# Moving an activation table's load behind the square root, telling a static schedule when stores land, and splitting the last stores over two queues

## The chip, the cores and the metric

The kernel runs on one core of one Trainium2 chip. The metric is the device time of one execution in microseconds (us). Its engines are TensorE (PE in the profile; PEld for its weight loads), VectorE (DVE), ScalarE (ACT), GpSimd (POOL) and SyncE (SP), which here issues DMAs. Each runs its own instructions in program order and waits for the others through semaphores.

## The reference

An attention block of the RWKV kind gives `x` (3072 tokens of 384 features); a normalised SwiGLU block follows. Only the second part matters here:

```python
rms = np.sqrt(np.mean(x * x, axis=-1, keepdims=True) + 1e-06)
xn = x / rms * rms_g
g = xn @ w_gate
silu = g * (1.0 / (1.0 + np.exp(-g)))
val = xn @ w_val
return (silu * val @ w_out).astype(np.float32)
```

So for each block of tokens a square root is wanted once, and SiLU many times.

## The kernel before

The sequence is cut into 12 chunks, s = 0 to 11, and from the third on two are handled together. The kernel does not issue instructions in the order in which it is written. It first collects operations with an estimated cost, then places them with a list scheduler that knows each engine's order and the dependences, and issues them in the order of the planned starts. `land` is the time that passes after an operation until its result may be used. For the part up to about 240 us a random search over deadlines, with fixed seeds, looks for a good plan.

```python
def hop(self, before, after):
    a, b = self.ops[before][0], self.ops[after][0]
    return self.ops[before][4] + (self.HOP if a != b or a == "SP" else 0.0)   # [4] is land
...
for seed in range(4):
    rng, best, goals = random.Random(seed), None, dict(first)
```

ScalarE's square root and SiLU need different tables. The instruction that loads a table is put in by the compiler, ahead of the first activation that needs it:

```python
add("ACT", 3.1, [key], ["diag"],
    lambda bank=bank: act.activation(rms, bank[:, 0:NT], AF.Sqrt, scale=1.0 / DM, bias=eps), name=f"sqrt {s}")
```

The steady part is made of groups of seven matmul products, f1 to f7, in the PSUM banks a, b and c. SiLU reads bank a after f5; the next group's f1 may overwrite bank a only when VectorE's product h0 has read it too:

```python
mm(xs_b, a_keys, a, lambda: wb[i][:, o], lambda: xb[s], False, "f5")
add("ACT", 0.38, ["sums"] + a_keys, ["g0"], lambda: act.activation(late["gv"][:, 0, 0], a[:, 0, 0:NT], AF.Silu), name="silu0")
add("DVE", 0.42, a_keys + ["g0"], [f"h{m}.0"], lambda: dve.tensor_mul(h[:, 0], a[:, 1, 0:NT], late["gv"][:, 0, 0]), name="h0")
```

Beside this, ScalarE checks that all weights lie in a range ("look"). A check loads raw weights into half of `rows_out`, the buffer in which the results of the second layer wait for their stores, and runs two activations on them. So its load has to wait until an earlier store has read the buffer:

```python
keys = [f"r{2 * turn['look'] + i}" for i in range(2)]
add("SP", 0.95, [], keys, lambda: sp.dma_start(out=raw, in_=...), land=2 * LAND, name=f"look {n}")
add("ACT", 0.57, [], keys, lambda: act.activation(hi, hi, AF.Abs), name=f"look {n}")
add("ACT", 0.81, [], keys + ["seen"], lambda: act.activation(hi, hi, AF.Relu, ..., accum_out=seen[:, n : n + 1]), ...)
```

The stores themselves, and the flag `bad` that every engine reads at the end to branch around a general version of the kernel:

```python
queue, issue = ("ACT", act) if k > 1 and s + 2 == NS else ("SP", sp)
...                                       # give(): two DMAs, one for each half of the partitions
add(queue, 1.2, [f"r{k}"], ["stored"], give, name="store")
...
add("DVE", 0.2, [key], ["bad"], lambda: dve.tensor_copy(bad, bank[0:1, 0:1]), name="flag")
add("ACT", 0.6, ["bad", "stored"], [], load, name="flag")
```

## Time and profile before

| | before |
|---|---|
| time, median of the first 3 runs | 633.1 us |
| TensorE busy / waiting | 610.8 / 15.9 us |
| waits of TensorE before 60, 60 to 260, 260 to 600, after 600 us | 7.26, 1.56, 6.31, 0.80 |
| from the end of VectorE's last addition to the end | 5.96 us |

The waits are the idle times of TensorE in front of each of its matmuls, added up. (The view of waits leaves out idle times up to 0.15 us; the sums have them.) In the profile a line names first the group or instruction, then its busy time, and behind the last bar or in brackets the idle time of the engine before it and what ended that idle time. "PE bank_a <- DVE h" is TensorE, about to write bank_a, waiting for VectorE's instruction that writes h. The group of table loads, from the groups of ScalarE by form, with count, busy time, mean duration in ns, and idle time before:

```profile
L92 ACT ACT_TABLE_LOAD x22 | 28.2, 1283 | 4.8 <-PE bank_a L92 3.7 <-PEq L1661 0.8
```

There are 22 loads of 1.28 us each: one at the start, and one in front of each change between square root and SiLU.

### The profile page before, as it was taken

Reading aid. Unit: us, or ns where it says so; the run is one execution under the profiler, and the core shown is the slowest. Engines: PE = TensorE matmul, PEld = TensorE weight load, DVE = VectorE, ACT = ScalarE, POOL = GpSimd, SP = SyncE. Lnnn points to the kernel's source line nnn. Section 1 sums busy time; section 2 is a strip of 40 time slices with the busy share of each in tenths; the row PEclk is TensorE's granted clock in tenths of the full one; section 3 lists DMA queues with packets and bytes.
Section 4 is the critical chain, followed back from the end, with each engine's and each line's share of the span. In section 5 each row is a group of like instructions: output and inputs, shape, how many; then the busy total and the mean of one; then the engine's idle time right before and its main releaser. Section 6 shows DMA issues by size and latency. Waiting matters only on the chain.

```text
span 633.1 us, 15313 instructions
## 1 busy us (share of the span) xinstructions
PE 610.8 (96%) x6540; PEld 538.8 (85%) x6540; DVE 439.5 (69%) x621; ACT 353.2 (56%) x895; POOL 42.0 (7%) x41
## 2 busy tenths in 40 slices
PE   8979999999999999999999899999899999899995
PEld 8867787866888899888899788899788899788995
DVE  7787888798865797667795447896456876355641
ACT  6794878276495343945965552877443773232200
POOL 2243323200000000000000000000000000000000
PEclk9998999999999999999999899999999999999999
DMA  8676743115510312352311514131434011300001
GB/s 295 220 273 205 236 141 110 69 56 153 198 33 26 100 48 77 81 188 71 94 68 40 161 52 151 40 119 32 125 102 127 32 35 33 100 26 2 1 13 44
DMA packets 22782, 62.92 MB, mean 99 GB/s; under 512 B 3152, under 2 KB 10160, under 8 KB 21296
## 3 DMA queue, kind: packets, MB, share of 16 engines
q1 hardware_dynamic: 22128, 61.46, 30.8%
q8 instruction: 53, 0.87, 0.6%
q10 hardware_dynamic: 576, 0.39, 0.3%
q14 instruction: 25, 0.20, 0.1%
HBM read 55.94 MB, written 4.72 MB: 96 GB/s over the span
## 4 chain that ended last, share of the span: by engine, by line
PE 84%; ACT 6%; DMA 5%; DVE 3%; issue 1%; SPq 1%; ACTq 0%; DVEq 0%
PE bank_b L92 27%; PE bank_a L92 24%; PE bank_c L92 22%; PE at L92 10%; DMA out_dram<-rows_out 2%; DMA rows_out<-in_wot_dram 1%; ACT MO L92 1%; ACT ME L92 1%; DMA TOK<-in_tok_dram 1%; DVE rows_out L92 1%; DMA chan<-in_chan_dram 1%; SPq L92 1%; ACT L92 1%; DVE h L92 0%; ACT ulp L92 0%
## 5 line engine op out<-in xcount | busy, mean ns | idle before, releaser
L92 DVE TENSOR_TENSOR gv<-bank_b,m 128x512 f32<-128x512 f32 x90 | 62.1, 690 | 71.5 <-PE bank_b L92 67.4
L92 ACT ACTIVATE rows_out<-rows_out 128x384 f32<-128x384 f32 x72 | 40.0, 556 | 33.7 <-DMA rows_out<-in_wot_dram 14.9
L92 PE MATMUL bank_a<-xa,wa 64*128 64x256 f32 x396 | 50.7, 389 | 6.6 <-DVE h L92 6.6
L92 PE MATMUL bank_b<-xa,wa 64*128 64x256 f32 x444 | 54.6, 378 | 0.9 <-DVE gv L92 0.9
L92 ACT ACTIVATE gv<-gv 128x512 f32<-128x512 f32 (+1 forms) x60 | 30.6, 521 | 35.2 <-DVE gv L92 34.8
L92 PEld LDWEIGHTS bank_a<-xa,wa 64*128 64x128 f32 x396 | 37.8, 189 | 14.2 <-DVE h L92 8.3
L92 DVE TENSOR_TENSOR gv<-bank_c,gv 128x512 f32<-128x512 f32 x60 | 41.4, 691 | 12.1 <-PE bank_c L92 11.0
L92 PE MATMUL bank_a<-wo,h 128*128 128x192 f32 (+1 forms) x264 | 49.4, 343 | 0.0
L92 ACT ACTIVATE ME<-dmask,du 64x64 f32<-64x64 f32 x176 | 46.2, 331 | 4.4 <-DVE du L92 3.7
L92 PEld LDWEIGHTS bank_b<-xa,wa 64*128 64x128 f32 x444 | 42.4, 187 | 7.3 <-DVE gv L92 1.7
L92 PE MATMUL bank_a<-xb,wb 64*128 64x256 f32 x396 | 48.2, 376 | 0.0
L92 ACT ACTIVATE MO<-dmask,du 64x64 f32<-64x64 f32 x176 | 46.6, 336 | 0.8
L92 PEld LDWEIGHTS bank_a<-wo,h 128*128 128x128 f32 x264 | 43.5, 190 | 3.6 <-issue 0.3
L92 ACT ACTIVATE gv<-bank_a 128x256 f32<-128x256 f32 x30 | 11.5, 383 | 60.7 <-PE bank_a L92 60.5
L92 PE MATMUL bank_b<-t,wb 64*128 64x256 f32 x360 | 45.0, 382 | 0.0
L92 PE MATMUL bank_b<-t,s 64*128 64x256 f32 x360 | 44.8, 382 | 0.0
L92 PE MATMUL bank_c<-t,s 64*128 64x256 f32 x360 | 44.5, 379 | 0.3 <-DVE rows_out L92 0.3
L92 PE MATMUL bank_c<-xb,s 64*128 64x256 f32 x360 | 43.9, 376 | 0.0
L92 PEld LDWEIGHTS bank_a<-xb,wb 64*128 64x128 f32 x396 | 38.3, 187 | 4.4
L92 ACT COPY m<-bank_a 128x512 f32<-128x512 f32 (+1 forms) x35 | 19.9, 568 | 37.8 <-PE bank_a L92 37.0
L92 PEld LDWEIGHTS bank_c<-t,s 64*128 64x128 f32 x360 | 34.3, 187 | 6.4 <-issue 1.2
L92 PEld LDWEIGHTS bank_b<-t,s 64*128 64x128 f32 x360 | 35.2, 190 | 4.4
(152 smaller groups left out, 1257.4 us busy)
## 6 DMA issues: line engine op xcount, KB each, us to landing
chan<-in_chan_dram SPq DMA_DIRECT2D x11, 1024.0 KB, 5.1
TOK<-in_tok_dram SPq DMA_DIRECT2D x11, 768.0 KB, 5.1
VS<-in_vpad_dram SPq DMA_DIRECT2D x24, 256.0 KB, 4.0
raw<-in_wot_dram SPq DMA_DIRECT2D x8, 576.0 KB, 4.6
rows_out<-in_wka_dram SPq DMA_DIRECT2D x12, 384.0 KB, 3.2
rows_out<-in_wkb_dram SPq DMA_DIRECT2D x12, 384.0 KB, 3.3
rows_out<-in_wot_dram SPq DMA_DIRECT2D x12, 384.0 KB, 3.3
out_dram<-rows_out SPq DMA_DIRECT2D x42, 96.0 KB, 2.3
```

Source lines behind the costliest of these rows:

```text
L92: return lambda *args, **kwargs: self.tc.keep_in_program_order(give(*args, **kwargs))
```

## The change

The intent has three parts: (1) a SiLU of one column right behind each square root, so that SiLU's table is loaded there and not in front of the first SiLU that TensorE waits for, with a plan that knows that the square root's result is ready 1.5 us before the pair ends; (2) a landing time of 2.5 us for stores in the plan; (3) each of the last block's stores split over SyncE's and ScalarE's queues, and the flag written behind the last addition.

```diff
+    TABLE = 1.5
+    def silu_table():
+        act.activation(spare, eps, AF.Silu)
...
-            add("ACT", 3.1, [key], ["diag"],
-                lambda bank=bank: act.activation(rms, bank[:, 0:NT], AF.Sqrt, scale=1.0 / DM, bias=eps), name=f"sqrt {s}")
+            def roots(bank=bank):
+                act.activation(rms, bank[:, 0:NT], AF.Sqrt, scale=1.0 / DM, bias=eps)
+                silu_table()
+            add("ACT", 3.3, [key], ["diag"], roots, land=-TABLE, name=f"sqrt {s}")
...                                       # likewise for the square root of two columns of s == 0
-            add(queue, 1.2, [f"r{k}"], ["stored"], give, name="store")
+            if s + 2 == NS:
+                add("SP", 0.6, [f"r{k}"], ["stored"], lambda: give((0,), sp), land=2.5, name="store")
+                add("ACT", 0.6, [f"r{k}"], ["stored'"], lambda: give((1,), act), land=2.5, name="store")
+            else:
+                add("SP", 1.2, [f"r{k}"], ["stored"], lambda: give((0, 1), sp), land=2.5, name="store")
...
-        add("DVE", 0.2, [key], ["bad"], ...)
-        add("ACT", 0.6, ["bad", "stored"], [], load, name="flag")
+        add("DVE", 0.2, [key, "r1"], ["bad"], ...)
+        add("ACT", 0.6, ["bad"], [], load, name="flag")
```

More of the change, by code (lines that the diff above doesn't have):

```diff
@@ L858, in mixing @@
             )
-            add(
-                "ACT", 3.1, [key], ["diag"],
-                lambda bank=bank: act.activation(rms, bank[:, 0:NT], AF.Sqrt, scale=1.0 / DM, bias=eps), name=f"sqrt {s}",
-            )
+            def roots(bank=bank):
+                act.activation(rms, bank[:, 0:NT], AF.Sqrt, scale=1.0 / DM, bias=eps)
+                silu_table()
+            add("ACT", 3.3, [key], ["diag"], roots, land=-TABLE, name=f"sqrt {s}")
             add("DVE", 1.75, [], ["diag"], lambda: dve.reciprocal(rms, rms), name=f"inv {s}")
@@ L871, in mixing @@
             if quick:
-                add("ACT", 0.3, [key], ["ms"], lambda bank=bank: root(bank, ms[:, 0]), name=f"sqrt {s}")
+                add(
+                    "ACT", 0.3 + TABLE, [key], ["ms"], lambda bank=bank: [root(bank, ms[:, 0]), silu_table()], land=-TABLE,
+                    name=f"sqrt {s}",
+                )
                 add("DVE", 0.15, [], ["ms"], lambda: dve.reciprocal(ms[:, 0], ms[:, 0]), name=f"inv {s}")
@@ L1096, in result, with give @@
         def result(k, chunk, f, js=(0, 1)):
-            queue, issue = ("ACT", act) if k > 1 and s + 2 == NS else ("SP", sp)
-            def give():
-                for bl in range(2):
+            def give(bls, issue):
+                for bl in bls:
                     to = bass.AP(
@@ L1164, in flag @@
         )
-        add("DVE", 0.2, [key], ["bad"], lambda: dve.tensor_copy(bad, bank[0:1, 0:1]), name="flag")
-        add("ACT", 0.6, ["bad", "stored"], [], load, name="flag")
+        add("DVE", 0.2, [key, "r1"], ["bad"], lambda: dve.tensor_copy(bad, bank[0:1, 0:1]), name="flag")
+        add("ACT", 0.6, ["bad"], [], load, name="flag")
     t_sum = lambda s, n, reads, writes: add(
```

## The prediction

> **What bounds the kernel now.** I read the page first: busy times, then the chain that ended last.
>
> ```profile
> span 633.1 us, 15313 instructions
> PE 610.8 (96%) x6540; PEld 538.8 (85%) x6540; DVE 439.5 (69%) x621; ACT 353.2 (56%) x895; POOL 42.0 (7%) x41
> PE 84%; ACT 6%; DMA 5%; DVE 3%; issue 1%; SPq 1%; ACTq 0%; DVEq 0%
> ```
>
> TensorE (PE) is busy for 610.8 of 633.1 us and holds 84% of the chain. The change removes no matmul. It can give back only what lies between and behind them: 633.1 - 610.8 = 22.3 us. The view of waits, restricted to TensorE, splits most of that:
>
> ```profile
> PE bank_a L92 <- DVE h L92: 6.6, 4, 2.2
> PE at L92 <- ACT sq L92: 2.5, 3, 1.3
> PE at L92 <- DVE ME L92: 2.2, 1, 2.2
> ...
> PE bank_b L92 <- DVE gv L92: 0.9, 1, 0.9
> PE bank_c L92 <- DVE bad L92: 0.8, 1, 0.8
> ```
>
> Together with start-up waits (1.5, 1.1) and one of 0.3, the waits sum to 15.9 us; the other 6.3 us follow the last matmul, which ends at 626.75. I looked up each wait in the list of instructions. "bank_a <- DVE h" stands at 144.36 (1.23 us), 354.50 (2.23), 453.61 (1.59) and 552.20 (1.59); "bank_b <- DVE gv" at 458.66 (0.90). The three late bank_a waits have one cause, shown in the timeline of 351 to 354.6:
>
> ```profile
> 351.06 1.15 ACT L92 ACTIVATE rows_out<-rows_out 128x384 f32<-128x384 f32 x2 [5.92 <-DMA rows_out<-in_wot_dram]
> 352.11 0.18 ACT L92 ACTIVATION_READ_ACCUMULATOR rows_out<-rows_out 128x1 f32 x1
> ...
> 352.31 1.28 ACT L92 ACT_TABLE_LOAD   x1
> ...
> 353.61 0.38 ACT L92 ACTIVATE gv<-bank_a 128x256 f32<-128x256 f32 x1
> 354.02 0.42 DVE L92 TENSOR_TENSOR h<-bank_a,gv 128x256 f32<-128x256 f32 x1 [4.17 <-ACT gv L92]
> ...
> 354.50 0.51 PE L92 MATMUL bank_a<-xa,wa 64*128 64x256 f32 x2 [2.23 <-DVE h L92]
> ```
>
> The SiLU's operand in bank_a was complete when the f5 product ended at 349.69. ScalarE could not take it. First in its order stood a check of weights ("look", which goes through rows_out), idle 5.92 us for its load; then SiLU's table, 1.28 us. Only then came SiLU, VectorE's product h, and the matmul that may overwrite bank_a. Two further products (f6, f7: 349.52 to 352.27) hid the first 2.6 us of this; 2.23 us were not hidden.
>
> Why was the load late? The SyncE part of the timeline from 340 to 360:
>
> ```profile
> 344.10 1.25 SPq L92 DMA_DIRECT2D out_dram<-rows_out  x2
> 347.14 0.33 SPq L92 DMA_DIRECT2D rows_out<-in_wot_dram  x1
> 347.57 1.94 SPq L92 DMA_DIRECT2D out_dram<-rows_out  x2
> ```
>
> The check's load overwrites a buffer that a store still reads. The store was issued at 344.10 to 345.34 and the load had to wait for its landing, until 347.14; it landed at 350.96. The kernel orders its own instructions by a plan made when it is built, and in that plan a store is done as soon as it is issued (landing time 0). So the plan put the check ahead of the SiLU, and an in-order engine obeys.
>
> **What the Trainium skill says.** "ScalarE: Activation LUTs", section "What ACT_TABLE_LOAD costs": about 1283 ns for a table load, 2.66 us with its drain, for each switch to another set. The trace has 22 loads with a mean of 1283 ns, which agrees; a 1.38 us drain is not to be seen, since the load starts 0.01 to 0.02 us after the previous activation ends and the SiLU 0.02 us after the load. I use 1.28. "DMA: Bandwidth & Descriptors", "Issuing engines are not separate DMA queues": two issuing engines save only the sequencer's issue time. Here one store costs SyncE a median of 604 ns of issue, so about 0.6 us is what a second queue can save. "Runtime: NRT & Kernel Launch", "Instruction fetch mechanics": a taken branch to an instruction outside the window waits for a fetch. The trace agrees at the end: SyncE's branch at 628.37 is followed by its next instruction at 631.13, 2.76 us later.
>
> **Part 1, SiLU's table behind each square root.** There are 11 square roots in the run (one of two columns, ten of 256). Each is already followed, sooner or later, by a SiLU, and a square root always lies between two SiLU phases, so the number of loads stays at 22. Added are 11 SiLUs of one column; the comparable one-column square root took 0.20 us, so 11 x 0.2 = 2.2 us on an engine that is 44% idle. What moves is the load, from in front of the first urgent SiLU to a place behind the square root. VectorE's reciprocal needs only the square root, and the change tells the plan so (it ends TABLE = 1.5 us before the pair). Gain: where the load was on TensorE's path. That is 1.28 us at each of 354, 453 and 552: 3.84 us. At 99.5, 145, 303, 403 and 502 the load already came directly or one step behind the square root with TensorE never idle: nothing. At 206 and 231 it was late but hidden: nothing. In the start, the first SiLU's load at 40.39 pushed the squares for the mean by 1.28 us, and TensorE then waited 1.34 us for them at 43.64. Moving it to 22 gives up to 1.28 back, but there it delays a weight conversion on ScalarE (21.84) by about 1.5 us. That stretch is ordered by a random search that will be run anew, so I count half: 0.6.
>
> **Part 2, stores with landing time.** With 2.5 us per store (the measured median to landing is 2.3), a check's load and its two activations move later in the plan, behind the SiLU. What is left of the three waits without the table is 2.23 - 1.28 = 0.95, then 0.31 and 0.31; and the 0.90 at 458.66 hangs on a second check that waited 1.86 us for its load and pushed a SiLU and a copy. Sum 2.47. Parts 1 and 2 together remove 2.23 + 1.59 + 0.90 + 1.59 = 6.31. After that the SiLU should start just behind f5 and h be ready about 1.1 us after it, inside the 2.6 us of f6 and f7.
>
> **Part 3, the tail.** The last VectorE addition ends at 627.10. SyncE then issues two stores (627.13 to 627.60, 627.65 to 628.31) and branches at 628.37; from there to the end is 4.7 us of branch, semaphores and barrier. The last landing, 630.09, lies before 631.13 and does not set the end. With one store per queue SyncE saves 0.71. But the flag `bad` is now written behind the last addition, so each engine reads it afterwards. On SyncE, that read took 0.77 and the register work behind it 0.4, from 625.91 to 627.08: until now in the shadow of the last matmuls. New: store until 627.6, read until 628.4, branch at about 628.8. Net cost about 0.4 us. The 0.80 wait at 624.49 I leave: the second half of the last product overwrites a bank that VectorE had read until 624.44, which the change does not touch; the flag named there merely ended next to it.
>
> **Sum.** 633.1 - 6.3 - 0.6 + 0.4 = 626.6. A new order has small new collisions, as each of these orders had; I add 0.5: **627.1 us**, 0.9% less.
>
> **Rivals.** (a) *Only the table helps*: the checks stay in front because other deadlines rank them first; then 3.84 + 0.6 - 0.4 is left, about 629.1. For it: the plan's times drift from the chip's. Against: the added landing time of 2.5 us exceeds the 0.95 by which the check was late. (b) *ScalarE becomes the hold-up*: square root and two loads are now an unbroken 3.2 us, and a copy of bank_a (m1) or an exchange has to wait behind it. For: ScalarE had 4 to 8 us strings without a pause around 303 and 403, and DVE work waits for xb there. Against: the plan has always charged 3.1 us for the square root and now 3.3, and the real total is the same 22 loads. It would give back 1 to 3 us: 628 to 630. (c) *The reordered start or store queue costs more*: loads for the next block come later behind stores on the in-order SyncE. Against: DMA share is 25 to 30% there and the loads are issued tens of us ahead. Up to 2 us. (d) *Everything idle in the searched part goes as well* (1.23 at 144, part of the start): 625.
>
> **Range and chances.** 625.0 to 630.5 covers (a), (b) and (d). For more than 2% faster, 12.7 us would have to go, more than all 8.7 us of waits after 60 us together; for 2% slower, the new order would have to double TensorE's idle time. I give each 0.015.
>
> **What would show it.** Right: the waits "bank_a <- DVE h" after 300 us and the one at 458 are gone, TensorE's total wait is 8 to 10 us instead of 15.9, 22 table loads remain with a load and a 0.2 us SiLU on `spare` behind each square root, SyncE's branch comes about 1.7 us after the last addition (now 1.27). Wrong: new waits of TensorE for a copy of bank_a or xb behind the 3.2 us block (b), checks still in front of the SiLU (a), or more idle time before 150 us, which would be the search's doing.

## The result, and the profile after

The changed kernel took 625.25 us (median of 4 runs, 623.26 to 627.21) against 633.81 us (median of 4 runs) for the kernel before. The ratio is 0.9865 (95% interval 0.9829 to 0.9901), 1.4% less. Ratios here are the mean time of one kernel's runs over that of the other's in the same rounds, so not quite the ratio of the medians. The spread of one kernel's runs goes with the clock that TensorE was granted: the changed kernel took 627.21 us in the run with a mean clock of 0.990 and, in a later job, 621.84 in one with 0.997. A time of one run is therefore good to about 2 us, and most of what follows is read from the waits instead.

The page of the changed kernel, its span, busy times and shares of the chain that ended last:

```profile
span 623.5 us, 15334 instructions
PE 609.2 (98%) x6540; PEld 539.3 (87%) x6540; DVE 442.9 (71%) x621; ACT 354.6 (57%) x906; POOL 42.9 (7%) x41
PE 95%; ACT 3%; DVE 1%; issue 0%; ACTq 0%
```

TensorE is busy for 98% of a shorter span, and DMAs have vanished from the chain (5% before). The view of waits of the changed kernel, TensorE alone (in total, times, longest):

```profile
PE at L92 <- DVE ME L92: 2.2, 1, 2.2
PE at L92 <- ACT sq L92: 1.2, 2, 1.0
PE bank_c L92 <- issue: 1.1, 1, 1.1
PE bank_c L92 <- DVE pw L92: 1.1, 1, 1.1
PE bank_c L92 <- DVE rows_out L92: 0.8, 1, 0.8
PE bank_b L92 <- DVE gv L92: 0.8, 1, 0.8
```

The waits fell from 15.9 to 7.2 us. "bank_a <- DVE h" (6.6 us before) is not there at all. Between 260 and 600 us TensorE never waits. The place that answers to 351 to 354.6 of the kernel before (its lines are in the prediction), from ScalarE's timeline of 338 to 352:

```profile
343.89 0.56 ACT L92 COPY m<-bank_a 128x512 f32<-128x512 f32 x1
348.77 0.38 ACT L92 ACTIVATE gv<-bank_a 128x256 f32<-128x256 f32 x1 [4.32 <-PE bank_a L92]
350.80 0.63 ACT L92 ACTIVATE gv<-gv 128x512 f32<-128x512 f32 x1 [1.64 <-DVE gv L92]
351.33 0.55 ACT L92 ACTIVATE rows_out<-rows_out 128x384 f32<-128x384 f32 x1
```

SiLU now runs as soon as bank_a is complete: ScalarE idled 4.32 us for it, where before the bank waited for ScalarE. The check, the last line, has moved behind two SiLUs, and no table load is in sight; it stands behind the square root, 15 us earlier. The end of the span, by the instructions on `bad` and those at the branch (min/median/max ns, first and last start):

```profile
L92 DVE CAST bad<-at x1: 133/133/133, 616.7 to 616.7; 1x1 int32<-1x1 f32 x1
...
L1171 SPq TENSOR_LOAD <-bad x1: 897/897/897, 617.4 to 617.4; - x1
```

```profile
L1625 SPq COMPARE_BRANCH  x1: 45/45/45, 618.7 to 618.7; - x1
```

The read of the flag on SyncE, 0.90 us, now stands between the last store (616.85 to 617.34) and the branch. From the last addition (end at 616.82) to the end of the span are 6.64 us, 0.68 more than before.

The difference of the two spans, 633.1 - 623.5 = 9.6 us, adds up so: the waits between 260 and 600 us 6.31, those before 60 us 7.26 - 5.63 = 1.63, those between 60 and 260 us 1.56 - 0.79 = 0.77, less the longer end 0.68; the remaining 1.6 us is TensorE's busy time, 610.8 against 609.2. The mean clock is 0.993 in both, so this last term is not its mean. Over all the profiles the busy time lies between 606.9 and 611.8 us, so the two figures alone do not say whose it is; the starts of the matmuls do. In e2 below, TensorE has the same order of matmuls as in the kernel before. If from the start of every matmul all idle time before it is subtracted, what is left grows, in the kernel before against e2, by 0.27 us at each of the four late waits, and by 0.23 us at 360.8 and at 558.4, where no idle time is shown: 1.55 us. (A further 1.45 us, behind the wait at 354.5, goes with a clock halved from 354.8 to 358.2; in the changed kernel the clock is halved for 3.4 us longer near 44 instead.) e11 against the changed kernel, again with equal orders of matmuls, shows 0.27 us at each of its seven waits after 257 us. So here a pause of TensorE costs 0.27 us more than the idle time that the profile shows, and the 1.6 us are very nearly the late waits' too.

### The profile page after: what moved, and what is told of

Same layout as the page of the kernel before. It is cut to its first block, busy times and chain, and to the rows that moved or that the text cites. A ratio compares the mean times of both kernels' runs of the same rounds, so it can differ in the third digit from the quotient of the medians.

```text
span 623.5 us, 15334 instructions
## 1 busy us (share of the span) xinstructions
PE 609.2 (98%) x6540; PEld 539.3 (87%) x6540; DVE 442.9 (71%) x621; ACT 354.6 (57%) x906; POOL 42.9 (7%) x41
## 4 chain that ended last, share of the span: by engine, by line
PE 95%; ACT 3%; DVE 1%; issue 0%; ACTq 0%
PE bank_b L92 31%; PE bank_a L92 27%; PE bank_c L92 25%; PE at L92 11%; ACT MO L92 1%; ACT ME L92 1%; ACT ulp L92 0%; ACT yT L92 0%; ACT VS L92 0%; ACT xb L92 0%; ACT sq L92 0%; DVE rows_out L92 0%; DVE xa L92 0%; DVE gv L92 0%; ACT wk L92 0%
## 5 line engine op out<-in xcount | busy, mean ns | idle before, releaser
L92 PE MATMUL bank_a<-xa,wa 64*128 64x256 f32 x396 | 49.2, 381 | 0.0
L92 PE MATMUL bank_b<-wo,h 128*128 128x192 f32 (+1 forms) x168 | 39.6, 392 | 0.0
L92 PEld LDWEIGHTS bank_b<-t,wb 64*128 64x128 f32 x360 | 34.4, 187 | 5.6 <-DVE gv L92 1.5
```

Of the source, the lines that this page charges most:

```text
L92: return lambda *args, **kwargs: self.tc.keep_in_program_order(give(*args, **kwargs))
```

## The experiments

Twelve runs were made, two of them repeats (e10, e12). All gave correct results. The table gives TensorE's waits in the profile, in us, by stretch; the time from the last addition to the end; and the ratio of times to the kernel before.

| run | before 60 | 60 to 260 | 260 to 600 | after 600 | sum | end | ratio (95%) |
|---|---|---|---|---|---|---|---|
| before | 7.26 | 1.56 | 6.31 | 0.80 | 15.92 | 5.96 | 1 |
| changed | 5.63 | 0.79 | 0 | 0.79 | 7.22 | 6.64 | 0.9865 (0.9829 to 0.9901) |
| e10, changed again | 5.37 | 0.79 | 0 | 0.80 | 6.96 | 6.69 | 0.9850 (0.9819 to 0.9880) |
| e1, tables, same order | 5.20 | 1.25 | 5.14 | 0.80 | 12.39 | 5.83 | 0.9966 (0.9922 to 1.0011) |
| e11, tables with plan | 5.49 | 2.17 | 5.35 | 0.79 | 13.79 | 6.09 | 0.9993 (0.9956 to 1.0030) |
| e2, landing alone | 6.57 | 1.38 | 0 | 0.80 | 8.74 | 6.35 | 0.9879 (0.9847 to 0.9911) |
| e3, tail alone | 7.05 | 2.07 | 5.10 | 0.80 | 15.01 | 6.73 | 1.0002 (0.9971 to 1.0033) |
| e5, before, other seeds | 7.29 | 2.17 | 5.74 | 0.79 | 15.99 | 5.89 | 1.0001 (0.9942 to 1.0061) |
| e6, changed, other seeds | 5.83 | 1.95 | 0 | 0.80 | 8.57 | 6.77 | 0.9917 (0.9877 to 0.9956) |
| e4, flag early | 5.56 | 0.79 | 0 | 0.80 | 7.15 | 6.30 | 0.9837 (0.9790 to 0.9884) |
| e7, read behind first half | 5.45 | 0.79 | 0 | 0.80 | 7.04 | 5.52 | 0.9845 (0.9799 to 0.9890) |
| e12, e7 again | 5.63 | 0.79 | 0 | 0.80 | 7.22 | 5.55 | 0.9838 (0.9801 to 0.9876) |
| e8, own banks | 6.08 | 1.57 | 0 | 0.00 | 7.66 | 5.54 | 0.9822 (0.9778 to 0.9866) |
| e9, one SiLU | 6.04 | 2.11 | 0 | 0.79 | 8.94 | 5.72 | 0.9853 (0.9824 to 0.9883) |

### Which part removes the late waits: tables or landing times?

**e1_table_same_order** adds the SiLUs to the kernel before and leaves the plan's numbers alone, so that no other instruction moves:

```diff
-    lambda bank=bank: act.activation(rms, bank[:, 0:NT], AF.Sqrt, ...)
+    lambda bank=bank: [act.activation(rms, bank[:, 0:NT], AF.Sqrt, ...), silu_table()]
...                                       # likewise for the square root of two columns of s == 0
```

> The kernel before, with a SiLU of one column behind each of the 11 square roots and nothing else: the plan's costs are untouched, so every engine keeps the order of the kernel before (checked on the program: only the 11 activations and the places of the table loads differ). My accounting: the check still stands in front of the late SiLU, so 1.28 us of each of the three late waits of TensorE for h goes (2.23 to 0.95, 1.59 to 0.31, 1.59 to 0.31), the 0.90 behind the second check stays, and 1.28 of the start's wait at 43.6 goes. TensorE's waits fall from 15.9 to about 10.8 us, the time by 4 to 5 us to about 629. Rival (the parts overlap, the checks alone do it): the same here; it differs in the next run.

Measured: 630.55 us (median), the waits between 260 and 600 us only from 6.31 down to 5.14. The view of waits of TensorE shows that they have changed their name:

```profile
PE bank_b L92 <- DVE gv L92: 4.7, 3, 1.7
...
PE bank_a L92 <- DVE h L92: 1.3, 2, 0.9
```

The waits for h nearly went, more than I had expected, but 0.9 us of "bank_b <- DVE gv" became 4.7. The timeline of 342 to 355 of this run tells why:

```profile
347.72 0.36 ACT L92 ACTIVATE gv<-bank_a 128x256 f32<-128x256 f32 x1
...
350.73 1.14 ACT L92 ACTIVATE rows_out<-rows_out 128x384 f32<-128x384 f32 x2 [2.65 <-DMA rows_out<-in_wot_dram]
351.77 0.19 ACT L92 ACTIVATION_READ_ACCUMULATOR rows_out<-rows_out 128x1 f32 x1
351.86 0.92 ACT L92 ACTIVATE gv<-gv 128x512 f32<-128x512 f32 x2
...
352.68 0.56 ACT L92 COPY m<-bank_a 128x512 f32<-128x512 f32 x1
...
353.66 0.69 DVE L92 TENSOR_TENSOR gv<-bank_b,m 128x512 f32<-128x512 f32 x1
...
354.41 0.92 PE L92 MATMUL bank_b<-xa,wa 64*128 64x256 f32 x6 [1.66 <-DVE gv L92]
```

TensorE got through the first SiLU sooner and arrived sooner at the next obstacle: a second check, whose load had not become any earlier. ScalarE idled 2.65 us for that load, ran the check, two SiLUs and the copy m, and VectorE could free bank_b only then. What the table's load gave back, the second check took: of 6.31 us, 1.17 were gained.

**e2_landing_same_tables** gives landing times to the stores of all blocks but the last, and no SiLU:

```diff
-            add(queue, 1.2, [f"r{k}"], ["stored"], give, name="store")
+            add(queue, 1.2, [f"r{k}"], ["stored"], give, land=2.5 if s + 2 < NS else 0.0, name="store")
```

> The kernel before with the landing time of 2.5 us on every store except those of the last block, no added SiLU. In its program the late SiLU now stands in front of the check, with its table load in front of it. My recorded split (table 3.84, landing 2.47) taken as two separate gains: 1.28 of each late wait remains, waits fall by 2.5 us only, time about 631. Rival (the parts overlap): f6 and f7 give 2.6 us, and load, SiLU and product need 1.28 + 0.38 + 0.42 plus handovers = about 2.2, so all of the 6.31 us goes without any change to the tables; TensorE's waits fall to about 9.6 us and the time to about 627.

Measured: 625.75 us, and no wait at all between 260 and 600 us: all 6.31 us are gone without a changed table. With a ratio of 0.9879 the landing times alone give most of what the whole change gives (0.9865). Its timeline of 338 to 354:

```profile
344.76 0.59 ACT L92 COPY m<-bank_a 128x512 f32<-128x512 f32 x1 [3.53 <-PE bank_a L92]
...
345.37 1.28 ACT L92 ACT_TABLE_LOAD   x1
...
349.94 0.38 ACT L92 ACTIVATE gv<-bank_a 128x256 f32<-128x256 f32 x1 [3.29 <-PE bank_a L92]
350.36 0.42 DVE L92 TENSOR_TENSOR h<-bank_a,gv 128x256 f32<-128x256 f32 x1 [0.29 <-ACT gv L92]
```

SiLU's table is still loaded just in front of SiLU in program order. But with the check out of the way ScalarE has nothing to do there, and the load runs as soon as the copy m is done; it is over 3.29 us before SiLU's operand is complete. It had been on the path only because the check in front of it had pushed it there. The rival of this experiment holds in its result, though not quite in its reason: the load does not even need the 2.6 us that f6 and f7 give.

**e11_table_with_plan** is part 1 exactly as in the change, with its planned costs, and nothing else of it.

> The kernel before with part 1 of the change exactly (a SiLU behind each square root, plan cost 3.3 and the early release), landing times 0, tail as before. Theory after the runs so far: the checks stay in front, so after 300 us 4 to 5.5 us of waits remain as in e1_table_same_order (5.14), before 60 us about 5.5; total about 11.5 to 13, ratio about 0.995. Rival (my recorded split): only about 2.5 us of late waits remain, ratio about 0.991.

Measured: ratio 0.9993, not to be told from 1; waits of 5.35 us between 260 and 600 us. Of TensorE's waits, "bank_b <- DVE gv" is the largest:

```profile
PE bank_b L92 <- DVE gv L92: 6.5, 5, 1.5
```

Three of its five, of 1.4 to 1.5 us each, again follow a second check at 355, 453 and 551 us, and one of 1.37 at 257. My split is refuted by three runs: part 1 alone takes away 1.0 to 1.2 us of the late waits (in e11 nothing, if its wait at 257, just outside the stretch, is counted), not 3.84, and part 2 alone takes away 6.31, not 2.47.

### What the tables are worth

In the start, e1 keeps the order of the kernel before. There TensorE waited 1.34 us at 43.6 us for the squares that ScalarE handed over late. In e1 this wait is gone; in e2 (1.36) and e3 (1.35), where the first SiLU's load is not moved, it is there. The view of waits, first of e1, then of e2:

```profile
PE at L92 <- ACT sq L92: 1.2, 2, 1.0
```

```profile
PE at L92 <- ACT sq L92: 2.3, 3, 1.4
```

So the SiLU behind the very first square root is worth 1.3 us. With seeds 0 to 3 every engine has one order in all kernels up to about 55 us, apart from this SiLU and its load; the waits before 60 us are 6.57 to 7.26 us in the three runs without it (before, e2, e3) and 5.20 to 6.08 us in the nine with it. **e9_one_silu** keeps that one alone, with the landing times and the tail of e7 below:

```diff
-            def roots(bank=bank): ...           # square root and SiLU, cost 3.3, land=-TABLE
+            add("ACT", 3.1, [key], ["diag"], lambda bank=bank: act.activation(rms, ..., AF.Sqrt, ...), name=f"sqrt {s}")
```

> e7_read_behind_first_half with the added SiLU behind the first square root alone; the ten later ones have the plan's cost and the instructions of the kernel before. Theory after the runs so far (the landing time removes the late waits, one SiLU removes the start's wait of 1.3 us at about 43.6, the other ten do nothing for TensorE): TensorE's waits 7 to 8 us, none after 300 us but the 0.8 in the last product; ratio to the kernel before equal to e12_read_again within 0.3%. Rival (the ten SiLUs or the plan's knowledge of them are worth something after all): one or more waits of 0.5 us or more between 60 and 600 us beside what e12 has, ratio worse by over 0.3%.

Measured: ratio 0.9853 against 0.9838 for e12 in the same rounds; the difference of 0.15% is within the bound set, and within the intervals. After 260 us the waits are the same as in e12, so the ten later SiLUs do nothing there. But the rival's first half came true: a wait of 1.78 us at 142.8 us stands where e12 has 0.79 at about 162. It is not a new wait, but that of the kernel before at 144.36 (TensorE's timeline, first of the kernel before, then of e9):

```profile
144.36 1.57 PE L92 MATMUL bank_a<-xa,wa 64*128 64x256 f32 x12 [1.23 <-DVE h L92]
```

```profile
142.82 1.57 PE L92 MATMUL bank_a<-xa,wa 64*128 64x256 f32 x12 [1.78 <-DVE h L92]
```

Up to about 248 us e9 and e2 have the order of the kernel before, and all five runs of that order show this wait, from 0.92 (e1) to 1.78 us. The changed kernel and e11, in which the plan knows of the later SiLUs, share another order from about 55 us on, without it. That place lies in the part which the random search orders, and the next two runs ask how much of this is the search's luck.

**e5_before_other_seeds** and **e6_after_other_seeds** start the search from other seeds:

```diff
-        for seed in range(4):
+        for seed in range(4, 8):
```

> The kernel before with the plan's random search started from seeds 4 to 7 instead of 0 to 3, nothing else. It asks how much of the difference in the searched part (up to about 240 us) is the search's luck. Accounting: the three late waits with the checks in front stay (6 to 6.5 us with the one that follows); the waits before 240 us move by 1 to 2 us either way around 9.6; time 632 to 636. Rival (the part before 240 us improved because of the change itself): the waits before 240 us stay within 0.5 of 9.6.

> The changed kernel with seeds 4 to 7. Accounting: no wait after 300 us except the 0.8 in the last product; waits before 240 us 5 to 9 us (6.4 in the changed kernel); time 624 to 628. Rival: the waits before 240 us stay within 0.5 of 6.4, which would make them the change's own gain.

Measured: the kernel before gets 9.46 us of waits before 260 us instead of 8.82 (the 9.6 in my expectation is not what its trace shows), the changed one 7.78 instead of 6.42, both with waits at other places. The late waits follow the change and not the seed: 5.74 and 0. The time of e6, ratio 0.9917, is 0.5% worse than the changed kernel's 0.9865, but the intervals overlap, and its waits are only 1.4 us (0.2%) longer. One and the same order also varies from run to run: 8.82, 7.95 (e2) and 9.12 us (e3) before 260 us. So between 0 and 260 us a plan is good to about 1 us either way. The 1.3 us between 60 and 260 us by which e9 is behind e12 come with the other order, but with seeds 4 to 7 the two kernels differ there by 0.22 us only. Whether the ten later SiLUs, the plan's knowledge of them, or the search's luck earn it stays open. Neither form of my accounting nor of its rival held fully here: both before-kernels are above both changed ones, by 2.4 us with the first seeds and 1.7 with the others, so the gain is not constant to 0.5; with the first seeds 1.3 of it is shown to be the first SiLU's.

### The end

**e3_tail_only** applies part 3 alone, with landing times 0:

```diff
-            queue, issue = ("ACT", act) if k > 1 and s + 2 == NS else ("SP", sp)
+            # last block: give((0,), sp) and give((1,), act); other blocks: give((0, 1), sp)
-        add("DVE", 0.2, [key], ["bad"], ...)
-        add("ACT", 0.6, ["bad", "stored"], [], load, name="flag")
+        add("DVE", 0.2, [key, "r1"], ["bad"], ...)
+        add("ACT", 0.6, ["bad"], [], load, name="flag")
```

> The kernel before with only the tail of the change: each last store on two queues, the flag written behind the last addition, landing times 0, tables as before. Accounting: TensorE's waits as before (15.9 us); from the end of the last addition to the end of the span about 6.6 us instead of 5.96, as in the changed kernel (6.64); time +0.4 to +0.7 us, not to be told from noise in the rounds. Rival (two queues shorten the end): that stretch falls to about 5.3 us.

Measured: 6.73 us from the last addition to the end, as in the changed kernel (6.64 and 6.69), against 5.96; ratio 1.0002. The accounting holds: the tail of the change, two queues with the flag behind the last addition, costs 0.7 us. This run does not tell the two apart; e7 does. The 0.80 us wait in the last product stays, although the flag's cast has moved behind everything; so the name "bad" that the profile gave it in the kernel before was an accident.

**e4_after_flag_early** removes the flag's new dependence from the changed kernel:

```diff
-        add("DVE", 0.2, [key, "r1"], ["bad"], ...)
+        add("DVE", 0.2, [key], ["bad"], ...)
```

> The changed kernel without the flag's dependence on the last addition; the rest of every engine's order is the same (checked on the program). Accounting: the registers are read in the shadow of the last matmuls again, SyncE issues one store behind the last addition and branches at once, so the stretch from the last addition to the end falls from 6.64 to about 5.4 us, and the time by 1.2 us against the changed kernel, to about 624. Rival (the read is free where it is, or another engine's branch ends last): the stretch stays at 6.6.

Measured: the stretch is 6.30 us, not 5.4; a miss. The read itself went early: SyncE's began at 614.17. But the plan put it ahead of the remaining stores, and the store of the first half of the last result then waited for the last addition, so it must have stood behind it in the program's order. Its issue is recorded from 615.69 to 617.49, past the end of that addition at 616.76, although it does not need it. SyncE thus still had a second store to issue, from 617.60 to 618.13.

**e7_read_behind_first_half** puts the read between the stores of the first half and those of the second:

```diff
+                z = "last" if js == (1,) else "stored"
-                add("SP", 0.6, [f"r{k}"], ["stored"], lambda: give((0,), sp), land=2.5, name="store")
+                add("SP", 0.6, [f"r{k}"], [z], lambda: give((0,), sp), name="store")
...                                       # likewise for ACT
-        add("DVE", 0.2, [key, "r1"], ["bad"], ...)
-        add("ACT", 0.6, ["bad"], [], load, name="flag")
+        add("DVE", 0.2, [key], ["bad"], ...)
+        add("ACT", 0.6, ["bad", "stored", "stored'"], [], load, name="flag")
```

> The changed kernel with the flag cast and read between the first and the second half of the last product, behind the stores of everything but the last half; landing times of the last block's stores 0. In e4_after_flag_early the read stood in front of three stores, so a store was issued late and SyncE still had two to issue behind the last addition. Here SyncE has one. Accounting: read and register work end at about 616.5, before the last addition; the store takes 0.5 and the branch follows at about 0.6 us behind the addition (1.87 in the changed kernel); the stretch from the last addition to the end is about 5.4 us (6.64), time about 1.2 us less than the changed kernel, 624.0. Rival: another engine's branch or the last landing (about 2.4 us after issue) ends last, and the stretch stays above 6.

> e7_read_behind_first_half once more, in the same rounds as the changed kernel. The stretch from the last addition to the end is 5.5 us against 6.6, and nothing else differs in any engine's order, so the time should be 1.1 us (0.18%) below e10_changed_again. Rival (the difference of e7 to the changed kernel was the clock's): equal within 0.05%.

> The changed kernel as it stands, for a comparison in the same rounds: ratio to the kernel before 0.986 to 0.990, TensorE's waits about 7.2 us, 6.6 us from the last addition to the end.

Measured: 5.52 us (e7) and 5.55 us (e12) from the last addition to the end, 1.1 us less than the changed kernel; SyncE's branch ends 0.62 us behind the addition instead of 1.91. SyncE's read on `bad` in e7, early again:

```profile
L1172 SPq TENSOR_LOAD <-bad x1: 887/887/887, 613.6 to 613.6; - x1
```

In the kernel before, which also reads ahead of the last addition but has both last stores on SyncE, the branch ends 1.31 us behind it. So the second queue does save the predicted 0.7 us there; of this 0.4 us reach the end (5.52 against 5.96), since the way from the branch to the end took 4.90 us instead of 4.65. In the rounds shared by e10 and e12 the ratios are 0.9850 and 0.9838. The difference, 0.12%, has the expected sign and size (0.18% expected), but the intervals overlap widely, so it is the traces that show the gain, not the times.

**e8_own_banks** further gives the halves of the last product a bank each:

```diff
+            if s + 2 == NS:
+                own, keys["v"] = next_at()
+                flat["v"] = own[:, 0:DM].rearrange("p (j f) -> p j f", j=2)
...                                       # the flag's matmul in the free half of bank b, ahead of the last product
```

> The same, and each half of the last product in a PSUM bank (and tile) of its own, the flag in a third. Accounting: the 0.8 us wait of TensorE in front of the second half goes, since nothing that VectorE still reads is overwritten; the sum c22 starts right behind c21 instead of 0.73 us later (it reads the other bank of the tile that the last product writes). TensorE's waits 6.4 us, time 0.8 us less than e7_read_behind_first_half, about 623.2. Rival: the wait was for the flag's cast (the profile names it), which also is gone in front of the second half here; the two are told apart by e3_tail_only and the changed kernel, where the cast had moved behind and the 0.8 stayed: so if the wait stays here, neither was the cause.

VectorE's timeline at the end, first of the changed kernel, then of this run:

```profile
612.04 0.56 DVE L92 TENSOR_TENSOR rows_out<-bank_a,rows_out 128x384 f32<-128x384 f32 x1
613.33 0.82 DVE L92 TENSOR_TENSOR rows_out<-bank_c,rows_out 128x384 f32<-128x384 f32 x2 [0.73 <-PE bank_c L92]
616.46 0.36 DVE L92 TENSOR_TENSOR rows_out<-bank_c,rows_out 128x192 f32<-128x192 f32 x1 [2.31 <-PE bank_c L92]
```

```profile
613.36 0.56 DVE L92 TENSOR_TENSOR rows_out<-bank_a,rows_out 128x384 f32<-128x384 f32 x1
613.95 0.56 DVE L92 TENSOR_TENSOR rows_out<-bank_c,rows_out 128x384 f32<-128x384 f32 x1
614.43 0.14 DVE L92 CAST bad<-bank_b 1x1 int32<-1x1 f32 x1
614.84 0.36 DVE L92 TENSOR_TENSOR rows_out<-at,rows_out 128x192 f32<-128x192 f32 x1 [0.28 <-PE at L92]
616.79 0.36 DVE L92 TENSOR_TENSOR rows_out<-at,rows_out 128x192 f32<-128x192 f32 x1 [1.59 <-PE at L92]
```

In the changed kernel the sum on bank_c idles 0.73 us until TensorE's first half of the last product is done, though it reads the other bank of that tile; then it and the addition behind it (0.82 together) hold up the second half. With separate tiles it starts right behind its predecessor, and the 0.8 us wait of TensorE is gone. The second half's addition follows the first half's by 1.95 us instead of 2.67. The run removes two things at once, this delay of VectorE and the bank that both halves share, so it does not say how much of the 0.8 us each is worth. The ratio is 0.9822, the lowest, against 0.9845 for e7 in the same rounds. Two other waits of this run keep its sum from showing the gain: 1.50 us at 14.8, where e7 has 0.97, and 0.78 at 180, which does not occur in e7; the part of the program where they fall was not edited. So e8 is the version to keep, with the gain over e7 seen in the trace and not proved by the times.

## Why the prediction was right or wrong

The time was right: 627.1 us predicted with 625.0 to 630.5, 625.25 measured, at the lower edge; one of the four runs, 623.26, lies below it. In part this was luck: the medians fell by 8.6 us where 6.0 had been summed, and the largest term came out right although its split was wrong. Point by point:

- **The bound and the size of the late waits: right.** The four waits after 300 us went entirely, 6.31 us as summed, and these are two thirds of the change of span.
- **The split of that sum: wrong.** The step that failed is "Gain: where the load was on TensorE's path. That is 1.28 us at each of 354, 453 and 552: 3.84 us", and with it "What is left ... Sum 2.47". Part 1 alone is worth 1.0 to 1.2 us there (e1, e11) and part 2 alone 6.31 (e2). I had subtracted the load from a chain whose other link, the check, stayed; but TensorE then ran into the second check (3.8 us more of waits for gv in e1). And with the check gone the load is not on the path at all, since ScalarE is idle when it comes up. The sum came out right because it is the size of the waits and not of its two causes. Rival (a), that only the table helps, was the wrong way round: only the landing time helps late in the run.
- **The start: mechanism right, size too small.** I gave 0.6 for half of 1.28, because the search would be run anew; but it kept the order of this stretch up to about 55 us. The 1.34 us wait went entirely (e1). Altogether the waits before 60 us fell by 1.63.
- **Part 3: right in sign and mechanism, 0.4 expected, 0.68 measured.** The read took 0.90 us on SyncE instead of 0.77, and the branch began 1.86 us behind the addition where I had said 1.7. The 0.7 us that the second queue saves was right (e7).
- **The wait of 0.80: stays, as said.** The reason was half of it. The second half waits for VectorE, but VectorE was late, too, because a sum on the neighbouring bank had itself waited for the first half (gone in e8).
- **New collisions, +0.5: wrong sign.** Between 60 and 260 us there is one new wait of 0.79, and 1.56 us of old ones went. This is nearest to rival (d), which had given 625 for it: the wait at 144 and more than 0.6 us of the start went. What changed the order there is part 1's costs in the plan (e11 has it, e2 has not); whether by luck stays open.
- **The cost of a pause: too small.** I counted the late waits by their idle time, 6.31 us. By the comparison with e2 they cost TensorE about 1.55 us more, which the profile books as busy, and no term of mine covers it.

From the predicted -6.0 to the measured -9.6 us of span: -1.0 for the start, -1.3 between 60 and 260 us, +0.3 for the end and -1.6 for busy time make -3.6. Rival (b), ScalarE as the hold-up, did not occur: there is no wait of TensorE after 260 us in the changed kernel but the last product's.

## What to carry to other kernels

In a static plan, the landing time of a store matters to everything that reuses its buffer: one missing 2.5 us put a stalled operation ahead of the urgent one on an in-order engine, and cost 6.3 us. When two causes stand in one chain, test each alone before dividing the gain between them: the one nearer to the wait, the table load, was worth 1.0 to 1.2 of 6.3 us without the other and nothing with it. At the end of a program, look at what each queue does between the last result and its branch; moving a 0.9 us register read into the shadow of the last matmul was worth more (1.1 us) than a second queue (0.4 us). And where runs share an order, compare starts and not only idle times: here each pause cost 0.27 us more than its idle time.

## What the Trainium skill lacked or had wrong

- "ScalarE: Activation LUTs", "What ACT_TABLE_LOAD costs", gives 2.66 us for a change of table with its drain of about 1.38. In these runs the load took 1.28 us, began about 0.02 us after the activation before it had ended unless it waited for an operand, and the next activation began about 0.01 us behind it when its operand was ready. No further drain is to be seen.
- The same page does not say whether a load waits for the operand of the activation that needs it. Both occurred: in e2 the load ended 3.29 us before SiLU's operand came, in the kernel before the one at 210.42 us stood idle 3.67 us for bank_a first. What decides is open.
- "Runtime: NRT & Kernel Launch", "Instruction fetch mechanics", says that a taken branch can stall for a fetch and gives no figure. SyncE's next instruction came 2.77 us after its branch began in the kernel before and 2.85 us in the changed one; that a fetch takes this time is not shown.
- "DMA: Bandwidth & Descriptors", "Latency and other measured facts", gives about 600 ns as the floor of a register load. From an on-chip tile it took 0.47 us on SyncE in e4, and 0.90 us right behind the issue of a DMA in the changed kernel.
